# A cast of the second query tile on ScalarE, and new places for the work of a list scheduler, in a fused attention, feed-forward and expert kernel

## The chip, the cores and the metric

One core of a Trainium2 chip runs the whole program as one launch. A core has five engines that run side by side, each through its own instructions in the order in which the program gives them: TensorE (PE, matrix products; PEld are its weight loads), VectorE (DVE), ScalarE (ACT), GpSimd (POOL) and SyncE (SP, which here issues nearly all transfers). The DMA engines move the data. The metric is the device time of one execution in microseconds; the median of several runs is compared, lower is better.

## The reference

Three stages, each feeding the next:

```python
# 1. attention, batch 2, 8 heads, 576 tokens, head size 64, causal, with a bias from a running sum of s
cum = np.cumsum(np.maximum(s, 0.0), axis=-1)
bias = -(cum[:, :, :, None] - cum[:, :, None, :])
scores = np.where(causal, -1000000000.0, scale * np.matmul(q, k.transpose(0, 1, 3, 2)) + np.minimum(bias, 0.0))
attn = np.exp(scores - np.max(scores, axis=-1, keepdims=True))
x = np.matmul(attn / (np.sum(attn, axis=-1, keepdims=True) + 1e-09), v)      # 1152 tokens x 512
# 2. feed-forward, 512 -> 2048 -> 512
h = x @ w_in
x = (h * (1.0 / (1.0 + np.exp(-1.702 * h)))) @ w_out
# 3. eight experts: each token goes to the one with the largest logit, 512 -> 1024 -> 512 with relu
expert_idx = np.argmax(x @ w_gate, axis=1)
out[i] = gate_w[i] * (np.maximum(disp[e] @ w1[e], 0.0) @ w2[e])[pos[i]]
```

All inputs are float32. The kernel keeps most matrix products exact enough by splitting a number into a high and a low part and multiplying both.

## The kernel before, in words

Attention works on 8 head pairs x (2 batches of 4 pairs) and, in each pair, on 5 query tiles t: tile 0 has 64 rows, the others 128, and tile t sees 64 + 128 t keys. One `unit(x, t)` makes the scores of both heads of the pair on TensorE (`score_mm`, line 719, with the causal mask added at 720), their row maxima on VectorE, the exponentials `pexp` on ScalarE, and then splits `pexp` into two float16 parts in the tile `ph`: a cast gives the high part (`copy`, line 702 on ScalarE or 704 on VectorE, by the tuple PHA), and two subtractions on GpSimd (lines 764 and 769) give the low part. A DMA transpose on SyncE's queue (line 777) turns `ph` into `PT`; tiles 0 and 1 share the buffer `ph01` and one transpose. `av_unit` then multiplies PT with the split values V (line 797).

The operands of the scores lie in two buffers `QK[x % 2]`: rows 0 to 63 are the transposed k and q of the pair, made by `qk_T` from the loaded `kraw` and `qraw` (loaded by `qk_load`, line 667) with transposes on TensorE (688) and copies on ScalarE (694). Two further rows, 64 and 65, carry the running sums of s. For pair 0 they come straight from the prologue (`bias_rows`, line 535). The prologue also writes the sums of all pairs to `cum_d` in HBM (`bias_keep`, line 542), and for each later pair a small transfer in `qk_T` (line 677) reads them back into `QK`. `v_load` (594) loads v, `w_load` (358, 361) the weights of the dense stage, 512 KB at a time, three of them early.

The dense stage (`mm1`, `mm2`) begins inside attention and then fills TensorE alone; `w_conv` splits its weights. After it come routing (`logits`, `route`, `order`) and, for each expert, `w_unit` (weights), `xs_in`, `e_mm1`, `e_mm2` and `e_out`, which scatters the rows to the output.

The order of the work on every engine is made by the class `Plan`. Every step is given to `pl.op` with its engine, an estimate of its duration, what it reads and writes, and a rank. `Plan.run` plays the program with these estimates: on each engine, among the steps that are ready (or will be within 120 ns of the earliest), it takes the one with the lowest place, and this order is emitted. The place is the rank plus a number from the table `SHIFT`, which is looked up by a name made of the stage (a before rank 0, b0 to b4 for attention by rank modulo 5, b and c after it), the function, the engine and the buffer written. The rank in attention is 5 x + t. Transfers on SyncE and GpSimd are held back in this play while more than 3.18 us of earlier transfers are still to be done. The places change nothing in what is computed: dependencies hold under every order.

The ranks that the prediction speaks of: the v loads -20; `bias_keep` -9; `qk_load(1)` -10; `qk_load(2)` 2; the three early weight loads 1, 2 and 3; the bias rows of pair 1 and its transposes and copies 1; the transpose of tile t of pair x 5 x + t; the cast of tile 1 of pair x 5 x + 1.

Of the kernel before, what the change touches and what calls it, by code (L numbers as in the profile page):

```python
# [1610 lines left out]
```

## Time and profile before

| | us |
|---|---|
| median of 3 runs | 493.71 (492.6 to 497.37) |
| the profiled execution, its own time | 495.86 |
| its span, first to last instruction | 494.1 |
| TensorE busy in it | 465.5 |
| mean granted TensorE clock | 0.979 of 2.4 GHz |

The profile is of one execution; its times are microseconds from its first instruction. Matmuls overlap in the array, so that a busy TensorE is not one at its peak. The releaser of a wait is inferred, from the event that came last.

### The profile page before, as it was taken

How to read it: one execution, taken by the hardware profiler on the slowest of the kernel's cores; microseconds unless marked ns; L12 is line 12 of the kernel's file. 1: busy time of each engine (PE TensorE's matmuls, PEld its weight loads, DVE VectorE, ACT ScalarE, POOL GpSimd, SP SyncE). 2: the span in 40 equal slices, each digit the busy share in tenths (PEclk: the TensorE clock that was granted, in tenths of full speed). 3: DMA queues.
4: the chain of work that ended last, by engine and by line, in shares of the span. 5: the costliest groups of instructions: out<-in, count | busy, mean ns of one | idle time of the engine just before them, and what ended most of it. 6: DMA issues, size and time to landing. Idle time of an engine off the chain costs nothing.

```text
span 494.1 us, 9648 instructions
## 1 busy us (share of the span) xinstructions
PE 465.5 (94%) x3379; PEld 352.1 (71%) x3398; DVE 359.3 (73%) x817; ACT 328.6 (67%) x754; POOL 128.4 (26%) x136
## 2 busy tenths in 40 slices
PE   6599989999999999999999999999999999989993
PEld 5366666667677666766766966759688898878981
DVE  8867767888979988982324466846986879799980
ACT  3567878987557656673335346842886988899981
POOL 5616765867212222211000130002000110220250
PEclk9968989999999999999999999999999999999998
DMA  7997999978972554692000248821694687876820
GB/s 164 255 226 150 239 233 171 211 148 152 206 217 96 172 155 148 215 356 87 1 1 0 87 172 312 323 84 44 195 348 151 184 265 243 288 241 226 273 84 21
DMA packets 99047, 88.20 MB, mean 179 GB/s; under 512 B 66679, under 2 KB 77943, under 8 KB 98982
## 3 DMA queue, kind: packets, MB, share of 16 engines
q1 hardware_dynamic: 97108, 82.04, 61.3%
q0 software_dynamic: 1888, 5.52, 2.9%
q8 instruction: 27, 0.44, 0.4%
q14 instruction: 24, 0.20, 0.1%
HBM read 60.60 MB, written 14.19 MB: 151 GB/s over the span
## 4 chain that ended last, share of the span: by engine, by line
PE 49%; DMA 13%; DVE 12%; issue 10%; ACT 8%; POOL 5%; SPq 1%; POOLq 0%; DVEq 0%; ACTq 0%
PE SC L466 8%; PE SC L719 6%; PE MI L433 5%; DMA PT<-ph 5%; PE MX L433 4%; DMA out_dram<-x2R,small 4%; PE SC L467 3%; PE MI L437 2%; PE AV L1401 2%; PE AV L797 2%; PE MX L437 2%; DMA wraw<-in_moe_w_out_dram 2%; POOL ph L769 2%; PE MI L1372 2%; POOL ph L764 2%
## 5 line engine op out<-in xcount | busy, mean ns | idle before, releaser
L466 PE MATMUL SC<-woH,gtH 128*128 128x512 f32 x212 | 75.8, 481 | 0.0
L719 PE MATMUL SC<-QK 128*128 128x512 f32 (+4 forms) x192 | 65.1, 449 | 8.5 <-POOL ph L769 4.3
L447 DVE SCALAR_TENSOR_TENSOR gtH<-th,gtH 128x384 fp32r<-128x384 f32 x46 | 25.8, 561 | 40.0 <-ACT gtH L445 39.3
L764 POOL TENSOR_TENSOR ph<-pexp,ph 128x512 f16<-128x512 f32 (+4 forms) x32 | 44.7, 1398 | 31.8 <-DVE ph L704 26.3
L450 ACT ACTIVATE gtB<-th 128x384 bf16<-128x384 f32 x46 | 24.0, 521 | 37.1 <-PE SC L467 24.5
L433 PE MATMUL MI<-xT,wiH 128*128 128x384 f32 x216 | 47.0, 356 | 0.5 <-DVE th L443 0.4
L750 ACT ACTIVATE pexp<-SC,smA 128x192 f32<-128x192 f32 (+4 forms) x80 | 38.4, 520 | 12.7 <-DVE smA L741 9.2
L719 PEld LDWEIGHTS SC<-QK 128*128 128x128 f32 (+1 forms) x192 | 29.8, 197 | 23.1 <-issue 11.4
L466 PEld LDWEIGHTS SC<-woH,gtH 128*128 128x128 f32 x212 | 40.3, 194 | 3.2
L1295 DVE TENSOR_TENSOR wiL<-wraw,wiH 128x1024 bf16<-128x1024 f32 x32 | 38.9, 1221 | 3.7 <-ACT wiH L1294 3.5
L1295 DVE TENSOR_TENSOR woL<-wraw,woH 128x1024 bf16<-128x1024 f32 x32 | 38.9, 1218 | 3.1 <-ACT woH L1294 3.0
L1437 POOL DMA_INDIRECT out_dram<-x2R,small x8 | 9.9, 1240 | 119.1 <-ACT x2R L1464 82.5
L409 POOL TENSOR_TENSOR wiL<-wvi,wiH 128x512 bf16<-128x512 f32 x16 | 22.2, 1386 | 68.6 <-ACT wiH L405 64.2
L467 PEld LDWEIGHTS <-gtB 128*128 128x128 bf16 x138 | 13.2, 96 | 37.5 <-issue 37.2
L433 PEld LDWEIGHTS MI<-xT,wiH 128*128 128x128 f32 x216 | 37.8, 189 | 2.2 <-DVE th L443 0.9
L1118 POOL DMA_INDIRECT xs_d<-x2R,small x9 | 9.0, 996 | 112.9 <-DVE small L1058 57.3
L433 PE MATMUL MX<-xT,wiH 128*128 128x384 f32 x168 | 36.6, 358 | 0.1
L467 PE MATMUL SC<-woL,gtB 128*128 128x512 bf16 x94 | 36.7, 390 | 0.0
L1294 ACT ACTIVATE wiH<-wraw 128x1024 fp32r<-128x1024 f32 x32 | 33.6, 1055 | 1.9 <-DMA wraw<-in_moe_w_dram 1.4
L694 ACT ACTIVATE QK<-MI 64x288 f32<-64x288 f32 x57 | 24.1, 423 | 14.6 <-PE MI L688 9.0
L1294 ACT ACTIVATE woH<-wraw 128x1024 fp32r<-128x1024 f32 x32 | 33.5, 1055 | 0.4 <-DMA wraw<-in_moe_w_dram 0.4
L433 PEld LDWEIGHTS MX<-xT,wiH 128*128 128x128 f32 x168 | 29.6, 189 | 1.6 <-DVE th L443 0.8
(290 smaller groups left out, 1146.3 us busy)
## 6 DMA issues: line engine op xcount, KB each, us to landing
wraw<-in_moe_w_dram SPq DMA_DIRECT2D x64, 512.0 KB
wraw<-in_moe_w_in_dram SPq DMA_DIRECT2D x16, 512.0 KB
wraw<-in_moe_w_out_dram SPq DMA_DIRECT2D x16, 512.0 KB
xs_d<-x2R SPq DMA_DIRECT2D x16, 257.0 KB
kraw<-in_k_dram SPq DMA_DIRECT2D x8, 288.0 KB
qraw<-in_q_dram SPq DMA_DIRECT2D x8, 288.0 KB
out_dram<-x2R SPq DMA_DIRECT2D x9, 256.0 KB
x2R<-xs_d SPq DMA_DIRECT2D x8, 257.0 KB
```

The lines of the kernel that those rows point to most:

```text
L409: e_.tensor_tensor(out=dlo, in0=vi.bitcast(F32), in1=dhi.bitcast(F32), op=ALU.subtract)
L433: nc.tensor.matmul(ps, lhsT=whi[:, kc], rhs=xT[:, a, kc, cs], start=(kc == 0 and a == 0), stop=False)
L447: pl.op("dve", t_dve(CN), lambda: nc.vector.scalar_tensor_tensor(out=gh[:, 1], in0=th, scalar=0.5, in1=gh[:, 0].bitcast(F32), op0=ALU.mult ...
L450: pl.op("act", t_act(CN), lambda: nc.scalar.activation(out=gb, in_=th, func=AF.Copy, scale=0.5), r=[("th", n % 2)], w=[("gtb", gi)] + xw)
L466: nc.tensor.matmul(o, lhsT=gh[:, a, ts], rhs=whi, start=(fc == 0 and a == 0), stop=False)
L467: nc.tensor.matmul(o, lhsT=gb[:, ts], rhs=wlo, start=False, stop=(fc == NFC - 1))
L694: pl.op("act", t_act(3 * TQ, False) + 130, lambda o=o, in_=in_, sc=sc: nc.scalar.activation(out=o, in_=in_, func=AF.Copy, scale=sc), r=[bk ...
L719: nc.tensor.matmul(o[:rows, j0:j1], lhsT=t_[:, 2 * r, i0:i0 + rows], rhs=t_[:, 2 * r + 1, j0:j1], start=True, stop=False)
L750: pl.op("act", t_act(wdt, False, 1), lambda o=o, r=r, nm=nm: nc.scalar.activation(out=pe[:rows, r, :wdt], in_=o[:rows, :wdt], func=AF.Exp, ...
L764: pl.op(eng, (t_pool if eng == "pool" else t_dve)(n * T_), lambda rs_=rs_, e_=e_: e_.tensor_tensor(out=hl[:, rs_, 0:T_], in0=pe[:rows, rs_ ...
L1294: pl.op("act", t_act(1024), lambda: nc.scalar.activation(out=dhi, in_=raw, func=AF.Copy), r=[rk], w=kh, rank=rank, after=after)
L1295: pl.op("dve", t_dve(1024), lambda: nc.vector.tensor_tensor(out=dlo, in0=raw, in1=dhi.bitcast(F32), op=ALU.subtract), r=[rk, ks[0], ks[2]] ...
```

## The change

Two things change. PHA becomes (0, 1), so that the cast of tile 1 is done by ScalarE with `activation(Copy)` instead of VectorE with `tensor_copy`, once in each of the 8 pairs. And the table SHIFT is replaced: 255 entries become 377. Nearly every name has another number, and 122 entries have a suffix: a step's place is now its rank plus the entry of its name plus the entry of name and group, where the group of an attention step is its pair (`@0` to `@7`; `@x` for those with a rank of 40 or more) and that of a later step its rank divided by 12. Entries lie between -40 and 40 as before.

```diff
-    "a.bias_keep.sp.cumd": 3.9, "a.bias_rows.sp.QKb": -7.7, "a.consts.a.pool.identF": -19.5, "a.consts.b.pool.": 13.3,
...
-    "a.qk_T.act.QK": 9.4, "a.qk_T.dve.QK": -10.1, "a.qk_T.tr.pe.BK": 13.3, "a.qk_load.sp.raw": -15.6,
-    "a.v_load.sp.vraw": 14.3, "a.v_scale.dve.gtb": 34.4, "a.v_scale.dve.scl": 37.3, "a.v_scale.pe.BK": 16.3,
...
-    "b0.w_conv.top.act.wvi": -13.9, "b0.w_load.load.sp.wraw": 1.9, "b1.av_unit.pe.BK": 18.8, "b1.copy.dve.ph": 4.7,
-    "b1.qk_T.act.QK": -11.3, "b1.qk_T.sp.QKb": 24.3, "b1.qk_T.tr.pe.BK": -14.1, "b1.unit.act.pexp": -10.7,
...
-    "b1.unit.sp.PT": 2.2, "b1.v_load.sp.vraw": 6.1, "b1.w_conv.both.dve.wvi": -7.6, "b1.w_conv.low.dve.wraw": -12.9,
...
-    "b1.w_conv.top.act.wvi": -18.2, "b1.w_load.load.sp.wraw": 0.4, "b2.av_unit.act.xT": 8.7,
...
-    "b2.qk_load.sp.raw": -2.1, "b2.unit.act.pexp": -17.7, "b2.unit.dve.nm": -20.1, "b2.unit.pe.BK": 0.6,
-    "b2.unit.pool.phl": 14.7, "b2.unit.pool.phz": 32.1, "b2.unit.sp.PT": -19.6, "b2.v_load.sp.vraw": 2.3,
...
-    "b2.w_load.load.sp.wraw": 37.2, "b3.av_unit.pe.BK": 16.7, "b3.copy.dve.ph": -40, "b3.unit.act.pexp": -40,
...
-    "b3.unit.pool.phl": -19.8, "b3.unit.pool.phz": 18.2, "b3.unit.sp.PT": 35.9, "b3.v_load.sp.vraw": 19.8,
...
-    "b3.w_load.load.sp.wraw": 5.1, "b4.av_unit.act.xT": 12.4, "b4.av_unit.dve.ri": -3, "b4.av_unit.dve.xTl": 7.4,
...
-    "b4.unit.pe.BK": -0.8, "b4.unit.pool.phl": -30.2, "b4.unit.pool.phz": -22, "b4.unit.sp.PT": 39,
...
+    "a.bias_keep.sp.cumd": -10.7, "a.bias_rows.sp.QKb": -25, "a.consts.a.pool.identF": -16.4,
...
+    "a.qk_load.sp.raw": -13, "a.v_load.sp.vraw": 11.9, "a.v_scale.dve.gtb": -5.4, "a.v_scale.dve.scl": -24.6,
...
+    "b0.w_conv.top.act.wvi": 24.6, "b0.w_load.load.sp.wraw": -10.8, "b1.av_unit.pe.BK": -36.6, "b1.copy.act.ph": 39.5,
+    "b1.copy.act.ph@5": -8.7, "b1.qk_T.act.QK": -13.3, "b1.qk_T.act.QK@0": -13.3, "b1.qk_T.act.QK@2": 9.1,
...
+    "b1.qk_T.sp.QKb": -1.3, "b1.qk_T.tr.pe.BK": -31.4, "b1.qk_T.tr.pe.BK@1": 21.5, "b1.unit.act.pexp": -13.4,
...
+    "b1.unit.pool.phl@5": 17.6, "b1.unit.pool.phz": -11.2, "b1.unit.sp.PT": -17.2, "b1.v_load.sp.vraw": 10.5,
...
+    "b1.w_load.load.sp.wraw": -11.6, "b2.av_unit.act.xT": 22, "b2.av_unit.dve.ri": 3.9, "b2.av_unit.dve.ri@4": 2.9,
...
+    "b2.qk_load.sp.raw@3": 18.9, "b2.qk_load.sp.raw@4": 3.6, "b2.unit.act.pexp": -21, "b2.unit.dve.nm": 16.6,
...
+    "b2.unit.pool.phz@1": -22, "b2.unit.sp.PT": 19.9, "b2.v_load.sp.vraw": -9.4, "b2.w_conv.both.dve.wvi": -8.4,
...
+    "b2.w_conv.sign.dve.wvi": 0.7, "b2.w_conv.top.act.wvi": -28, "b2.w_load.load.sp.wraw": 21.5,
+    "b2.w_load.load.sp.wraw@0": 17.2, "b3.av_unit.pe.BK": 26.9, "b3.av_unit.pe.BK@3": 31.2,
...
+    "b3.unit.sp.PT": 1.2, "b3.unit.sp.PT@1": 1.2, "b3.v_load.sp.vraw": 10.3, "b3.v_load.sp.vraw@2": 15.7,
...
+    "b3.w_load.load.sp.wraw": 14.9, "b4.av_unit.act.xT": 24.2, "b4.av_unit.act.xT@2": 17.9, "b4.av_unit.dve.ri": -12,
...
+    "b4.unit.pool.phz@6": 8.2, "b4.unit.sp.PT": 17.1, "b4.v_load.sp.vraw": -8.4, "b4.w_conv.both.dve.wvi": -19.6,
...
         if rank is None:
             rank = self.rank
-        rank += SHIFT.get(self.name(eng, fn, w, rank), 0.0)
+        name = self.name(eng, fn, w, rank)
+        rank += SHIFT.get(name, 0.0) + SHIFT.get(name + self.group(name, rank), 0.0)
...
+    def group(self, name, rank):
+
+        return {"a": "@", "b": f"@{int(rank // 5)}" if rank < 40.0 else "@x", "c": f"@{int(rank // 12)}"}[name[0]]
...
     XTB = "act"
     AVG = (0, 3)
-    PHA = (0,)
+    PHA = (0, 1)
```

The entry of `b2.qk_load.sp.raw` in the new table is 15.3.

## Rows read from the trace of the kernel before

**Rows 1.** The page, part 1: busy time, share, instructions of each engine.
```profile
PE 465.5 (94%) x3379; PEld 352.1 (71%) x3398; DVE 359.3 (73%) x817; ACT 328.6 (67%) x754; POOL 128.4 (26%) x136
```

**Rows 2.** Busy time by stretch: stretch, length, engines (x instructions), granted clock, DMA, GB/s.
```profile
0.00:12.00 12.00, 7.93 (x68) 6.59 (x69) 9.87 (x22) 4.16 (x10) 6.73 (x25) 1.00 0.78 162
12.00:140.00 128.00, 115.69 (x1120) 80.50 (x1120) 101.49 (x217) 96.54 (x221) 74.25 (x71) 0.93 1.00 200
140.00:337.50 197.50, 196.93 (x1044) 139.49 (x1057) 125.29 (x267) 108.29 (x209) 23.99 (x21) 1.00 0.43 147
337.50:475.00 137.50, 134.28 (x1084) 117.83 (x1084) 116.24 (x295) 113.12 (x293) 20.58 (x16) 1.00 0.69 227
475.00:494.10 19.10, 10.63 (x77) 7.71 (x76) 6.40 (x18) 6.49 (x24) 2.89 (x3) 0.90 0.07 26
```

**Rows 3.** Waits of TensorE, 12 to 140 us: us in total, times, longest.
```profile
PE SC L719 <- POOL ph L769: 4.3, 1, 4.3
PE AV L797 <- DMA PT<-ph: 3.0, 4, 1.1
```

**Rows 4.** TensorE in order of time: start, us, what [idle before, releaser].
```profile
8.84 0.56 PE L719 MATMUL SC<-QK 128*128 128x192 f32 x2 [1.33 <-DMA QK<-QK]
...
19.89 0.47 PE L688 MATMUL MI<-identF,qraw 96*128 96x96 f32 x3 [0.64 <-ACT QK L694]
24.68 0.98 PE L719 MATMUL SC<-QK 128*128 128x192 f32 x2 [4.32 <-POOL ph L769]
```

**Rows 5.** ScalarE in order of time: the copies of q of the first head.
```profile
20.50 0.85 ACT L694 ACTIVATE QK<-MI 64x288 f32<-64x288 f32 x2
```

**Rows 6.** SyncE's queue in order of time.
```profile
13.46 0.44 SPq L358 DMA_DIRECT2D wraw<-in_moe_w_in_dram  x1
14.00 1.93 SPq L777 DMA_TRANSPOSE PT<-ph  x1
15.99 0.56 SPq L358 DMA_DIRECT2D wraw<-in_moe_w_in_dram  x1
16.66 1.68 SPq L677 DMA_DIRECT2D QK<-cum_d  x1
```

**Rows 7.** Instructions of line 677: duration in ns, least, median, most.
```profile
L677 SPq DMA_DIRECT2D QK<-cum_d x7: 261/298/1680, 16.7 to 95.9; - x7
```

**Rows 8.** Busy time by stretch, 4 us each, columns as in rows 2.
```profile
12.00:16.00 4.00, 4.00 (x18) 1.98 (x17) 3.60 (x9) 1.32 (x4) 1.62 (x2) 1.00 1.09 292
16.00:20.00 4.00, 2.85 (x18) 1.75 (x17) 3.44 (x10) 3.33 (x8) 3.54 (x4) 1.00 1.50 253
20.00:24.00 4.00, 0.36 (x3) 0.17 (x3) 3.47 (x6) 2.51 (x5) 2.89 (x3) 0.84 0.78 207
```

**Rows 9.** Busy time by stretch around the slow clock, columns as in rows 2.
```profile
23.00:24.00 1.00, 0.00 (x0) 0.00 (x0) 1.00 (x1) 0.00 (x0) 1.00 (x2) 0.50 1.09 286
31.00:32.00 1.00, 1.00 (x4) 0.55 (x2) 0.88 (x2) 0.96 (x4) 0.00 (x0) 0.50 1.14 185
33.00:34.00 1.00, 1.00 (x38) 1.00 (x35) 0.49 (x2) 0.00 (x0) 0.00 (x0) 1.00 1.32 241
43.00:47.00 4.00, 4.00 (x30) 3.31 (x30) 2.59 (x7) 2.15 (x7) 2.50 (x2) 0.57 0.87 203
70.00:74.00 4.00, 4.00 (x39) 3.39 (x39) 2.50 (x6) 1.48 (x5) 2.50 (x2) 0.57 1.27 265
```

**Rows 10.** Groups by line and shape, 0 to 145 us: busy us, mean ns, idle before.
```profile
L704 DVE CAST ph<-pexp 128x384 f16<-128x384 f32 x8 | 3.0, 377 | 0.4 <-ACT pexp L750 0.4
L702 ACT ACTIVATE xTb<-xT 128x320 bf16<-128x320 f32 x8 | 3.8, 470 | 0.3
L702 ACT ACTIVATE xTb<-xT 128x256 bf16<-128x256 f32 x8 | 3.3, 417 | 0.3
```

**Rows 11.** The page, part 4: shares of the chain that ended last.
```profile
PE 49%; DMA 13%; DVE 12%; issue 10%; ACT 8%; POOL 5%; SPq 1%; POOLq 0%; DVEq 0%; ACTq 0%
```

**Rows 12.** Busy time, 60 to 100 us, columns as in rows 2.
```profile
60.00:100.00 40.00, 35.70 (x382) 25.10 (x380) 31.15 (x75) 33.58 (x77) 27.78 (x25) 0.96 1.07 205
```

More of the change, by code (lines that the diff above doesn't have):

```diff
@@ L23 @@
 SHIFT = {
-    "a.bias_keep.sp.cumd": 3.9, "a.bias_rows.sp.QKb": -7.7, "a.consts.a.pool.identF": -19.5, "a.consts.b.pool.": 13.3,
-    "a.consts.dve.identB": -28.5, "a.consts.dve.ones1": 13.2, "a.consts.dve.ph": 22.6, "a.consts.dve.vss": 9.9,
-    "a.consts.pool.QKb": 1.4, "a.consts.pool.V2o": 22.6, "a.prologue.dve.cum": 6.7, "a.prologue.dve.neg": 5.3,
-    "a.prologue.dve.one": 16.1, "a.prologue.dve.one2": 25.2, "a.prologue.dve.s": 22, "a.prologue.sp.s": -32.6,
-    "a.qk_T.act.QK": 9.4, "a.qk_T.dve.QK": -10.1, "a.qk_T.tr.pe.BK": 13.3, "a.qk_load.sp.raw": -15.6,
@@ L29 @@
-    "a.v_load.sp.vraw": 14.3, "a.v_scale.dve.gtb": 34.4, "a.v_scale.dve.scl": 37.3, "a.v_scale.pe.BK": 16.3,
[3 rows of a table removed]
-    "b.w_conv.low.dve.wraw": -28.8, "b.w_conv.main.act.wo": -6.4, "b.w_conv.rest.dve.wo": -25.6,
-    "b.w_conv.rest.pool.wo": 9.4, "b.w_conv.sign.dve.wvi": -7.6, "b.w_conv.top.act.wvi": 21.5,
[38 rows of a table removed]
-    "c.evac.dve.x2r": -1.4, "c.expert.ld.sp.eid": -39.6, "c.first_early.dve.sel": 28.3, "c.first_early.mm.pe.BK": 3.6,
-    "c.first_load.load.sp.x2r": 2.4, "c.first_rows.dve.sel": 7.1, "c.first_rows.pe.BK": -23.5, "c.keep.pool.": 14.7,
@@ L75 @@
-    "c.keep.sp.": 12.5, "c.logits.act.x2T": 10.4, "c.logits.dve.ix": -4.3, "c.logits.dve.lg": 9.3,
-    "c.logits.dve.mx": 23.7, "c.logits.dve.x2T": -33.3, "c.logits.mm.pe.BK": -39.3, "c.logits.pe.BK": -21.9,
-    "c.mm1.act.gt": 9.5, "c.mm1.act.gtb": -5.4, "c.mm1.act.th": 25.2, "c.mm1.dve.gtl": -9.1, "c.mm1.dve.th": 6.7,
-    "c.mm1.pe.BK": -24.6, "c.mm2.mm.pe.BK": -17.6, "c.order.dve.base0": -4.2, "c.order.dve.ov": 13.3,
-    "c.order.dve.srt": 31.1, "c.pool.iotaW": 16.2, "c.route.act.w8": 9.2, "c.route.count.pe.BK": -31.8,
@@ L80 @@
-    "c.route.dve.cnt": 26.7, "c.route.dve.gate": -28.3, "c.route.dve.idx": -23.8, "c.route.dve.oc": -5.1,
-    "c.route.dve.oh": 11.4, "c.route.dve.pos": 17.9, "c.route.dve.rel": -28.6, "c.route.dve.sb": -20.2,
-    "c.route.dve.se": 0.4, "c.route.dve.slot": -28.1, "c.route.dve.t3": 35.2, "c.route.dve.tok": -21.3,
-    "c.route.dve.w8": -37.5, "c.route.scatter.pool.xs": -26.9, "c.send.scatter.pool.": -8.7,
-    "c.w_conv.both.dve.wvi": -25.3, "c.w_conv.low.dve.wraw": -5.6, "c.w_conv.main.act.wi": 18.5,
@@ L85 @@
-    "c.w_conv.main.act.wo": 10.2, "c.w_conv.rest.dve.wo": 14.8, "c.w_conv.rest.pool.wi": -11.5,
-    "c.w_conv.sign.dve.wvi": 20.1, "c.w_conv.top.act.wvi": 29.1, "c.w_load.load.sp.wraw": 22.9,
-    "c.w_unit.act.wi": 18.2, "c.w_unit.act.wo": 22.4, "c.w_unit.dve.wi": 7.8, "c.w_unit.dve.wo": 6.2,
-    "c.w_unit.load.sp.wraw": -0.7, "c.xs_first.act.xsT": -14.6, "c.xs_first.act.xsTb": -2.9,
-    "c.xs_first.dve.xsTb": 19.9, "c.xs_first.dve.xsTl": -0.3, "c.xs_first.load.sp.meta": -23.2,
-    "c.xs_in.act.xsT": -21.8, "c.xs_in.act.xsTb": 21.1, "c.xs_in.dve.meta": -18.5, "c.xs_in.dve.xsTl": 9.8,
@@ L91 @@
-    "c.xs_in.load.sp.x2r": -38.7, "c.xs_in.tr.pe.BK": -1.5, "c.zero.pool.zrow": -8.2, "c.zeros.sp.out0": -1.9,
-    "c.zeros.sp.xs0": 2.5,
+    "a.bias_keep.sp.cumd": -10.7, "a.bias_rows.sp.QKb": -25, "a.consts.a.pool.identF": -16.4,
+    "a.consts.b.pool.": -18.8, "a.consts.dve.identB": -8.4, "a.consts.dve.ones1": 3.2, "a.consts.dve.ph": 13.4,
+    "a.consts.dve.vss": 4, "a.consts.pool.QKb": -9.4, "a.consts.pool.V2o": -2.1, "a.prologue.dve.cum": 20.1,
+    "a.prologue.dve.neg": -8.5, "a.prologue.dve.one": -8.2, "a.prologue.dve.one2": 9.6, "a.prologue.dve.s": -19.4,
@@ new lines @@
+    "a.prologue.sp.s": -15, "a.qk_T.act.QK": 23.5, "a.qk_T.dve.QK": 8, "a.qk_T.tr.pe.BK": -17.9,
+    "a.qk_load.sp.raw": -13, "a.v_load.sp.vraw": 11.9, "a.v_scale.dve.gtb": -5.4, "a.v_scale.dve.scl": -24.6,
[3 rows of a table added]
+    "b.w_conv.both.dve.wvi": 19.4, "b.w_conv.low.dve.wraw": -8.3, "b.w_conv.low.dve.wraw@x": -22.1,
+    "b.w_conv.main.act.wo": -8.2, "b.w_conv.rest.dve.wo": -6.1, "b.w_conv.rest.pool.wo": 0.8,
+    "b.w_conv.sign.dve.wvi": 2.2, "b.w_conv.top.act.wvi": -5.9, "b.w_load.load.sp.wraw": 22.3, "b0.copy.act.ph": 30.1,
[59 rows of a table added]
@@ new lines @@
+    "c.first_early.mm.pe.BK": 39, "c.first_load.load.sp.x2r": 17.8, "c.first_rows.dve.sel": 12.7,
+    "c.first_rows.pe.BK": 8.9, "c.keep.pool.": 21, "c.keep.sp.": -10.7, "c.logits.act.x2T": 19.3,
[7 rows of a table added]
+    "c.route.count.pe.BK@2": 7.6, "c.route.dve.cnt": 3.7, "c.route.dve.gate": 3.1, "c.route.dve.idx": -17.9,
+    "c.route.dve.oc": -23, "c.route.dve.oh": -14.4, "c.route.dve.oh@3": 6.5, "c.route.dve.pos": -9.7,
+    "c.route.dve.rel": 22.2, "c.route.dve.sb": -30.2, "c.route.dve.se": -32.5, "c.route.dve.se@3": 21.8,
@@ new lines @@
+    "c.route.dve.slot": -12.2, "c.route.dve.t3": -0.3, "c.route.dve.tok": -31.5, "c.route.dve.w8": -9.2,
+    "c.route.scatter.pool.xs": -18, "c.send.scatter.pool.": 14.1, "c.w_conv.both.dve.wvi": -13.4,
+    "c.w_conv.low.dve.wraw": 19.2, "c.w_conv.main.act.wi": 19.5, "c.w_conv.main.act.wo": -15.1,
+    "c.w_conv.rest.dve.wo": 2.7, "c.w_conv.rest.dve.wo@0": 23, "c.w_conv.rest.pool.wi": 12.4,
+    "c.w_conv.sign.dve.wvi": 24.9, "c.w_conv.sign.dve.wvi@0": -10.8, "c.w_conv.sign.dve.wvi@2": -35.2,
@@ new lines @@
+    "c.w_conv.top.act.wvi": 18.6, "c.w_conv.top.act.wvi@1": -11.6, "c.w_load.load.sp.wraw": -4.2,
+    "c.w_load.load.sp.wraw@1": -6.6, "c.w_unit.act.wi": 27.5, "c.w_unit.act.wi@11": 4.7, "c.w_unit.act.wi@7": 0.9,
+    "c.w_unit.act.wi@8": -15.2, "c.w_unit.act.wo": 39.6, "c.w_unit.act.wo@10": 16.6, "c.w_unit.dve.wi": 8.7,
+    "c.w_unit.dve.wi@11": 11.2, "c.w_unit.dve.wo": 3.3, "c.w_unit.load.sp.wraw": 8.1,
+    "c.w_unit.load.sp.wraw@4": -23.2, "c.w_unit.load.sp.wraw@6": 6.3, "c.w_unit.load.sp.wraw@7": 22,
@@ L93 @@
+    "c.xs_first.act.xsT": -12.9, "c.xs_first.act.xsTb": 26.4, "c.xs_first.dve.xsTb": 5.6, "c.xs_first.dve.xsTl": -1.6,
[6 rows of a table added]
 }
```

94 rows, old and new, of the table SHIFT are left out of this document.

## The prediction

> **What bounds the kernel now.** I read the page's first part, then the busy time in five stretches, then TensorE's waits, and last the order of time around the longest of them. The reader is to see that TensorE is at work for 465.5 of 494.1 us [rows 1], so that nearly all that an order can give back lies in its 28.6 idle us and in its slow stretches. The five stretches [rows 2] say where these are: start-up 4.1 us idle (12.00 - 7.93), attention 12.3 us (128.00 - 115.69), the dense stage 0.6 us, routing and experts 3.2 us, the end 8.5 us. Attention is also the only long stretch in which the granted clock is below 1: 0.93. So attention is the stage to look at. The dense stage after it hardly waits at all; what attention saves should therefore reach the end of the kernel.
>
> Of the waits inside attention one is far longer than the others: a score matmul waits 4.3 us, once; four waits for a transposed tile make 3.0 us [rows 3]. In order of time it is the first score matmul of the second head pair (x = 1): TensorE ends its last transpose at 19.89 + 0.47 = 20.36 us and starts again at 24.68 [rows 4]. The row names POOL as the releaser, yet a score matmul reads nothing that POOL has just written. Its operands are QK, written by ScalarE, which had the first head's last part ready at 20.50 + 0.85 = 21.35 us [rows 5], and the two bias rows, which one small transfer (line 677) brings from cum_d. The SyncE queue issues that transfer at 16.66 us, behind two weight loads and the first transpose [rows 6], and the issue itself takes 1680 ns where the median of the seven is 298 [rows 7]. By elimination I take the bias transfer as what ended the wait, about 8 us after its issue: it stood behind a backlog.
>
> The bytes agree. By the shapes in the code, in KB, 36 (s), 576 (k and q of pair 0), 1152 (v), 18 and 144 (cum rows), 576 and 576 (k and q of pairs 1 and 2), 1024 (two weight loads) and 256 (the first transpose) go ahead of it: 4358 KB, 4.46 MB. The transfers moved 1.94 MB by 12 us (12 x 162 GB/s [rows 2]), then 1.17, 1.01 and 0.83 MB in 4 us each [rows 8]; 4.46 MB is reached at 21.6 us. The wait ended at 24.68, some 3 us later.
>
> The Trainium skill, "DMA: Bandwidth & Descriptors", section Queues, rings and completion order, says that on each DMA engine the descriptors of a queue are consumed in ring order, so that a small transfer does not pass what is ahead of it there; the 8 us here agree. [...]
>
> **The change, part by part.**
>
> *Places of the early transfers.* A place is rank plus shift, the lower going first among what is ready. For the bias rows of pair 1 it goes from 1 + 24.3 = 25.3 to 1 - 1.3 = -0.3. The first weight load goes from 1.4 to -10.6, the third from 8.1 to 17.9, the second from 39.2 to 40.7 (2 + 21.5 + 17.2); k and q of pair 2 from -0.1 to 17.3. The writing of cum_d goes from -5.1 to -19.7, past the v loads (-5.7 to -8.1). So cum_d is written earlier, and the bias rows then stand behind one weight load instead of two and ahead of k and q of pair 2: 4358 - 576 - 512 = 3270 KB, 3.35 MB, reached at 16.95 us, or 3.09 MB at 15.9 us if the first transpose comes later too. With the same 3 us behind it they land between 18.9 and 20.0 us. Late next is ScalarE's copy of q, done at 21.35. The signal from TensorE to this copy took 0.14 us (20.36 to 20.50); with as much on the way back TensorE starts at 21.5 instead of 24.68, 3.2 us earlier. If the copy also comes earlier (its place falls from -10.3 to -25.6, ahead of most exponentials) it is up to the whole 4.3 us; if the transfer was not the cause, 0. I take -3.2.
>
> *The slow stretch behind the wait.* At the end of the idle time the granted clock is 0.50 (1.2 GHz), still so at 31 us, and 1.00 again at 33 [rows 9]; two score matmuls of 192 columns take 0.98 us there against 0.56 at full clock [rows 4]. TensorE works at most 7.8 us in it (24.68 to 32.5), which at 0.56/0.98 would be 4.5 us: 3.3 us to gain at most, nothing at least. The shorter gap that is left may still cost some clock, since behind waits of at most 1.1 us [rows 3] the clock fell too, to a mean of 0.57 over the 4 us from 43 and from 70 us [rows 9]. I take half: -1.6.
>
> *The cast of the second query tile.* Eight casts of 128x384 leave VectorE, 377 ns each, 3.0 us [rows 10]. On ScalarE no row has this size; copies of 320 and 256 elements take 470 and 417 ns, 0.83 ns an element, so 384 take about 523 ns, 8 x 0.523 = 4.2 us (estimate). All of it on the path would be +4.2, all of VectorE's on it -3.0. Weighted by the share of the chain that each engine has, 8% and 12% [rows 11], it is +0.34 - 0.36: 0. What hides it is that TensorE sets the pace; without that cover it costs up to 4.2 us.
>
> *Transposes and all other places in attention.* The transposes of t = 1, 3 and 4 move forward by 19.4, 34.7 and 21.9, that of t = 2 back by 39.5, k and q back by at least 17.4. The four waits for transposes are worth 3.0 us, and the slow stretches at 43 and 70 us another 2 x 4 x (1 - 0.57) = 3.4 [rows 9]: 6.4 us, to be gained or doubled. Forward and back nearly balance; I take -0.4.
>
> *Places in the dense and expert stages.* Nearly every name moves. There are 0.6 and 3.2 us to gain [rows 2], and an order that fits worse could lose as much again. I take -0.3.
>
> Sum: -3.2 - 1.6 + 0 - 0.4 - 0.3 = -5.5 us. The profiled execution took 495.86 us (its span of 494.1 and 1.8 around it), which gives 490.4; it lay 2.15 us above the median of 493.71, so against that median 488.2 us.
>
> **Rivals.**
>
> *The lead is eaten.* The DMA engines' share over attention is 1.00 [rows 2]. If transfers set the pace over the whole stage, an early start of pair 1 only waits longer later, at the transposes. For it: the share, 1.07 between 60 and 100 us [rows 12]. Against it: only 3.0 us of waits name a transfer. Then the time is 493. The Trainium skill ("Trainium Kernel Development and Optimization", section Key Constraints) states that all queues run on the same 16 DMA engines and interleave, so an order adds no bandwidth; by that rule this rival would hold wherever the engines are full.
>
> *The wait stays.* If POOL, as the row says, or something else ended it, the order on SyncE's queue changes nothing: 493.7.
>
> *The cast comes late (slower).* Its place on ScalarE is 1 + 39.5, behind nearly all that ScalarE has ready, and ScalarE is busy 33.58 of 40 us between 60 and 100 [rows 12]. Behind the cast wait POOL's subtractions of this tile, the transpose that serves t = 0 and 1, whatever SyncE has queued behind that, and TensorE's first attention-value matmuls. A cast of 0.52 us behind one piece of 0.9 us would be 1.4 us late in each of eight pairs: 11.4 us, less the 5.5 of the sum: 499.6. It decides from 5.5/8 = 0.7 us a pair on. Against it: a pair takes 16 us (128 us of attention over eight), and only a lateness that outlasts the work between the two pairs reaches TensorE.
>
> *More gaps close.* Half of attention's other 8 us of idle time and half of the experts' 3.2: 488.2 - 5.6 = 482.6.
>
> **How the numbers follow.** Forecast 0.42 (its own range 485.5 to 490.5), lead eaten 0.20, wait stays 0.07, cast late 0.16, more gaps close 0.15. About 1% is what a measurement of this kernel can tell from no change: 488.8 and 498.6. Of the forecast's 0.42 two thirds lie below 488.8, which with 0.15 makes 0.43 faster; of the late cast 0.15 lies above 498.6; the rest, 0.42, is within 1%. The range 481 to 496 leaves out the late cast and little below.
>
> **What would show it.** Right: in the new profile the bias rows' transfer is issued before 15 us and pair 1's first score matmul starts near 21.5, with an idle time before it of 1 to 1.5 us; the clock between 24 and 32 us is mostly 1; VectorE's eight 128x384 casts are gone and ScalarE has eight near 523 ns; attention's idle time is some 8 us. Wrong: a wait of 3 us or more remains there, waits for transposed tiles grow beyond 3.0 us in all, or TensorE's idle time between 140 and 475 us grows beyond 3.8 us.

## The result

The changed kernel took **488.88 us** (median of 13 runs, 487.55 to 494.02) where the kernel before, run beside it, took 494.06 us (median of 13, 491.76 to 500.02): ratio **0.9909, 95% interval 0.9885 to 0.9932**. In a second series it was 490.74 us against 494.08, ratio 0.9926 (0.9892 to 0.9959). So the gain is 3.7 to 4.5 us: clear of no change, just under 1%, and smaller than the 5.5 us of the sum. Some executions fell into a slower state, over 1.5% above the fastest of their kernel; ratios and intervals leave them out and medians do not, so that a ratio need not be the quotient of the two medians beside it. The profiled execution took 490.40 us, 488.7 of them its span.

**The profile after.** First the page's part 1 (busy time, share, instructions), then the five stretches, with the columns of rows 2. Lines of the kernel lie 36 further on: the scores are now L755, the bias transfer L713, the attention-value matmuls L833.

```profile
PE 460.2 (94%) x3379; PEld 349.9 (72%) x3398; DVE 358.2 (73%) x809; ACT 330.9 (68%) x762; POOL 128.2 (26%) x136
```

```profile
0.00:12.00 12.00, 8.39 (x72) 6.69 (x72) 8.69 (x21) 4.41 (x10) 6.87 (x25) 1.00 0.81 162
12.00:140.00 128.00, 114.67 (x1131) 79.84 (x1131) 107.32 (x217) 99.62 (x230) 71.46 (x71) 0.96 0.97 206
140.00:337.50 197.50, 196.26 (x1051) 140.32 (x1065) 121.37 (x275) 108.02 (x210) 24.26 (x21) 1.00 0.42 143
337.50:475.00 137.50, 134.93 (x1100) 119.25 (x1100) 118.85 (x293) 115.95 (x304) 23.76 (x18) 1.00 0.69 226
475.00:488.70 13.70, 5.94 (x38) 3.78 (x34) 1.94 (x7) 2.88 (x11) 1.85 (x2) 0.90 0.10 37
```

The reader is to see what did not change. TensorE's idle time is 488.7 - 460.2 = 28.5 us, against 28.6 before [rows 1]. Attention's is 13.3 us, against 12.3 [rows 2]. Nearly the whole difference between these two executions is in busy time: 5.3 us less, of which the granted clock accounts for at most (1 - 0.979) x 494.1 - (1 - 0.987) x 488.7 = 4.0; at most, because a slow clock costs nothing while TensorE waits.

Next, the place to which the prediction pointed. SyncE's queue, then TensorE, each in order of time:

```profile
11.46 0.45 SPq L394 DMA_DIRECT2D wraw<-in_moe_w_in_dram  x1
12.03 0.29 SPq L713 DMA_DIRECT2D QK<-cum_d  x1
```

```profile
20.70 0.47 PE L724 MATMUL MI<-identF,qraw 96*128 96x96 f32 x3 [1.04 <-ACT QK L730]
21.00 0.52 PE L755 MATMUL SC<-QK 128*128 128x192 f32 x2
...
23.99 0.32 PE L833 MATMUL AV<-V,PT 128*128 128x64 f16 x3 [1.80 <-DVE V L693]
```

The transfer is issued at 12.03 instead of 16.66 us [rows 6], pair 1's first score matmul starts at 21.00 instead of 24.68 [rows 4], without a wait. But 1.2 us later TensorE stands again, for 1.80 us, this time for V's split on VectorE. The waits between 12 and 140 us (us in total, times, longest) confirm it:

```profile
PE AV L833 <- DVE V L693: 3.7, 3, 1.8
PE AV L833 <- DMA PT<-ph: 2.8, 3, 1.4
```

In place of the 4.3 us of rows 3 there are now 3.7 us for V; the waits for transposed tiles are as before. The slow clock behind the wait got shorter, but did not go away (columns of rows 2; compare rows 9):

```profile
22.00:23.00 1.00, 0.19 (x2) 0.08 (x2) 1.00 (x1) 1.00 (x3) 1.00 (x1) 0.50 2.10 204
27.00:28.00 1.00, 1.00 (x19) 1.00 (x17) 1.00 (x3) 0.95 (x2) 0.00 (x0) 0.50 1.24 235
...
29.00:30.00 1.00, 1.00 (x28) 1.00 (x26) 1.00 (x2) 0.81 (x4) 0.00 (x0) 1.00 0.69 143
```

The casts are where they were expected, at 508 ns each (estimate 523), with no idle time of ScalarE before them:

```profile
L738 ACT ACTIVATE ph<-pexp 128x384 f16<-128x384 f32 x8 | 4.1, 508 | 0.0
```

From this profile alone one would say: forecast met, by the early transfer, but for attention's idle time, forecast at some 8 us. The experiments say otherwise.

### The profile page after: what moved, and what is told of

Same layout as the page of the kernel before. It is cut to its first block, busy times and chain, and to the rows that moved or that the text cites. A ratio compares the mean times of both kernels' runs of the same rounds, so it can differ in the third digit from the quotient of the medians.

```text
span 488.7 us, 9679 instructions
## 1 busy us (share of the span) xinstructions
PE 460.2 (94%) x3379; PEld 349.9 (72%) x3398; DVE 358.2 (73%) x809; ACT 330.9 (68%) x762; POOL 128.2 (26%) x136
## 4 chain that ended last, share of the span: by engine, by line
PE 65%; DVE 9%; DMA 8%; issue 6%; ACT 6%; POOL 3%; SPq 2%; POOLq 0%; DVEq 0%; ACTq 0%
PE SC L502 9%; PE AV L1437 7%; PE MI L469 5%; PE MX L469 5%; PE SC L503 4%; PE MI L1408 4%; PE MX L1408 4%; PE AV L1439 3%; DMA wraw<-in_moe_w_dram 3%; PE SC L755 3%; DMA PT<-ph 3%; PE AV L502 3%; PE MI L473 2%; PE MX L473 2%; POOL ph L800 2%
## 5 line engine op out<-in xcount | busy, mean ns | idle before, releaser
L755 PE MATMUL SC<-QK 128*128 128x512 f32 (+4 forms) x192 | 62.9, 432 | 4.0 <-ACT pexp L786 2.8
L786 ACT ACTIVATE pexp<-SC,smA 64x64 f32<-64x64 f32 (+4 forms) x80 | 37.9, 520 | 17.3 <-DVE smA L777 15.0
L502 PEld LDWEIGHTS SC<-woH,gtH 128*128 128x128 f32 x212 | 39.9, 194 | 3.0
L755 PEld LDWEIGHTS SC<-QK 128*128 128x128 f32 (+1 forms) x192 | 28.0, 186 | 16.3 <-issue 7.7
L833 PE MATMUL AV<-V,PT 128*128 128x65 f16 (+1 forms) x640 | 25.7, 197 | 6.5 <-DVE V L693 3.7
```

The source lines that it names most:

```text
L502: nc.tensor.matmul(o, lhsT=gh[:, a, ts], rhs=whi, start=(fc == 0 and a == 0), stop=False)
L755: nc.tensor.matmul(o[:rows, j0:j1], lhsT=t_[:, 2 * r, i0:i0 + rows], rhs=t_[:, 2 * r + 1, j0:j1], start=True, stop=False)
L786: pl.op("act", t_act(wdt, False, 1), lambda o=o, r=r, nm=nm: nc.scalar.activation(out=pe[:rows, r, :wdt], in_=o[:rows, :wdt], func=AF.Exp, ...
L833: nc.tensor.matmul(av[:, slot, r, 0:D + 1 - h_], lhsT=PT[t][:, r * (1 + 2 * t) + pb, :], rhs=rhs, start=(i == 0), stop=(i == len(m) - 1))
```

## The experiments

Twelve kernels in four series, each run 6 to 12 times beside the kernel before, whose median was 493.5 to 494.9 us.

| kernel | us | ratio to before (95%) |
|---|---|---|
| early_transfer: before + early transfer | 497.79 | 1.0035 (0.9999 to 1.0072) |
| cast_alone: before + cast on ScalarE | 495.65 | 1.0007 (0.998 to 1.0034) |
| attention_part: new places up to the end of attention | 492.48 | 0.9959 (0.9937 to 0.9981) |
| later_part: new places behind attention | 494.51 | 0.9997 (0.997 to 1.0024) |
| undo_early: changed, transfer late again | 489.55 | 0.9911 (0.9875 to 0.9946) |
| undo_cast: changed, cast on VectorE | 491.17 | 0.9939 (0.9905 to 0.9973) |
| undo_both: changed, both undone | 491.46 | 0.9950 (0.9922 to 0.9979) |
| unlock: changed, V split off POOL's subtraction | 491.02 | 0.9942 (0.9915 to 0.9968) |
| changed_again | 490.74 | 0.9926 (0.9892 to 0.9959) |
| first_pairs: new places up to pair 1 only | 499.44 | 1.0096 (1.0063 to 1.0128) |
| later_pairs: new places of pairs 2 to 7 only | 507.02 | 1.0224 (1.0177 to 1.0271) |
| routing_experts: new places of routing, experts only | 533.31 | 1.0747 (1.0708 to 1.0787) |

**One part alone, in the old order.** Two kernels keep every other instruction where the kernel before had it. In the first, a hook takes instructions out of the finished order; `put(n, m)` sets n right behind m:

```diff
+        put(at("sp", ("cumd", 0)), rows[1])
+        put(at("sp", ("cumd", 1)), at("sp", ("cumd", 0)))
...
+        put(loads[0], q1[3])
+        put(at("sp", ("QKb", 1, 0)), loads[0])
```

> The kernel before with every instruction in its old place but four steps of SyncE's queue: cum_d is written ahead of three v loads, and the first weight load and then the bias rows of pair 1 are issued ahead of k and q of pair 2 (the queue's order in the changed kernel, up to the first transpose). Theory 1 (this transfer carries attention's gain): pair 1's first score matmul starts near 21.5 us instead of 24.68 and the kernel is 2.5 to 4.8 us shorter, ratio 0.990 to 0.995. Theory 2 (the lead is used up by the second pair, as in the changed kernel, where it fell from 4.7 us at pair 1 to 1.2 us at pair 2, and attention's gain comes from other places): the first score matmul is early all the same, but the kernel is 0 to 1.2 us shorter, ratio 0.9975 to 1.000. If the wait stays near 24.7 us, the transfer was not its cause.

```diff
-            pl.op("dve", t_dve(n, True), lambda: nc.vector.tensor_copy(out=o, in_=i), r=r, w=w)
+            pl.op("dve", t_dve(n, True), lambda: nc.scalar.activation(out=o, in_=i, func=AF.Copy) if w[0] == ("ph", 1)
+                  else nc.vector.tensor_copy(out=o, in_=i), r=r, w=w)
```

> The kernel before with every instruction in its old order; only the eight 128x384 casts are issued on ScalarE, at the place in the whole order at which VectorE had them. My theory (what one engine gains the other loses, and TensorE sets the pace): within 1 us of before, ratio 0.998 to 1.002. Rival (VectorE is on the path behind the scores): up to 3.0 us shorter, ratio 0.994. Rival (the casts delay the exponentials behind them on ScalarE): 8 times 0.51 us = 4.1 us longer, ratio 1.008.

The cast moves nothing (+0.3 us, -1.0 to +1.7). The early transfer alone moves nothing or costs a little (+1.7 us, 0 to +3.6). Why it brings nothing is seen in the two traces side by side: TensorE in cast_alone, whose SyncE queue is the old one, then in early_transfer.

```profile
20.63 0.47 PE L688 MATMUL MI<-identF,qraw 96*128 96x96 f32 x3 [0.63 <-ACT QK L694]
23.23 0.56 PE L720 MATMUL SC<-QK 128*128 128x192 f32 x2 [2.14 <-DMA QK<-cum_d]
```

```profile
21.07 0.47 PE L710 MATMUL MI<-identF,qraw 96*128 96x96 f32 x3 [0.64 <-ACT QK L716]
22.63 0.56 PE L741 MATMUL SC<-QK 128*128 128x192 f32 x2 [1.09 <-issue]
```

The first row pair names the transfer as what ends the wait; that part of the reasoning holds. But the wait is 2.1 us here, 1.8 in later_part and 3.0 in later_pairs (below), whose queue up to this transfer is the same, not 4.3: the profile of before had caught a long one. With the transfer early, 1.09 us remain, ScalarE's copy of q (21.68 + 0.85 = 22.53 us) being what comes late next, as the prediction had it. The start moves by 0.4 to 0.6 us.

**One half of the places, by stage.** The cast and the table's entries for start-up and attention with the old entries behind them, and the converse:

```diff
+SHIFT = {k: v for k, v in CHANGED.items() if k[0] in "ab"}
+SHIFT.update({k: v for k, v in BEFORE.items() if k[0] == "c"})
```

CHANGED and BEFORE stand for the two tables, and in the kernel the result is written out; in the converse they change places, and the cast stays on VectorE.

> The changed kernel's cast and its places of start-up and attention, with the old places for the dense, routing and expert stages. In the changed kernel attention's end lies 3.1 us ahead of before, and the stages behind it give 2.3 us more. Theory A (the stages add up, since the dense stage hardly waits): 3.1 us shorter than before, ratio 0.9937, and no more. Theory B (an earlier and differently loaded end of attention is what the later stages gained from): the whole 5.4 us, ratio 0.989. Theory C (the later stages lose what attention gains without their own new places): ratio 0.998 or more.

> The other half: the old places of start-up and attention and the old cast, with the changed kernel's places for the dense, routing and expert stages. Theory A (the stages add up): 2.3 us shorter than before (dense -0.6, routing +1.0, experts +1.3, end +0.6), ratio 0.9953. Theory B (the later gain comes from attention's end): within 0.5 us of before, ratio 0.999 to 1.001. As predicted before the change ran it would be 0.3 us shorter.

Attention's places bring 2.0 us (0.9 to 3.1), a ratio between Theory A's and Theory C's that settles neither. Alone, the later ones bring nothing (Theory A's 0.9953 lies outside the interval), though routing and experts in that profile were as short as in the changed kernel: its dense stage was longer, and in the 4 us from 284 on its clock fell, which the changed kernel's did not (later_part, then the changed kernel; columns of rows 2).

```profile
284.00:288.00 4.00, 3.75 (x15) 2.44 (x15) 1.21 (x10) 0.60 (x1) 1.94 (x2) 0.63 0.53 199
```

```profile
284.00:288.00 4.00, 4.00 (x22) 2.56 (x21) 1.69 (x14) 0.82 (x2) 1.83 (x2) 1.00 0.53 198
```

**One part undone, in the new order.** The changed kernel's order with the bias rows late again; with the casts on VectorE; and with SyncE's whole start as in the kernel before and the casts on VectorE.

```diff
+        put(at("sp", ("QKb", 1, 0)), loads[1])
```

> The changed kernel with its order kept, except that the bias rows of pair 1 are issued behind the second weight load, as in the kernel before; their writing to cum_d stays early. Theory 1 (pair 1's early bias rows carry attention's gain): pair 1's first score matmul starts 1.5 to 3 us later than 21.5 us and the kernel is 2 to 3.3 us longer than the changed one, ratio to before 0.995 to 0.998. Theory 2 (what the early start gains is used up by pair 2; the earlier runs speak for it: the transfer alone gave 1.0035): the first score matmul is late all the same, but the kernel stays within 1 us of the changed one, ratio 0.989 to 0.993.

```diff
-            pl.op("act", t_act(n), lambda: nc.scalar.activation(out=o, in_=i, func=AF.Copy), r=r, w=w)
+            pl.op("act", t_act(n), lambda: nc.vector.tensor_copy(out=o, in_=i) if w[0] == ("ph", 1)
+                  else nc.scalar.activation(out=o, in_=i, func=AF.Copy), r=r, w=w)
```

> The changed kernel with its order kept, except that the eight 128x384 casts are issued on VectorE at the same place in the whole order. Theory (the engine of the cast doesn't matter while TensorE sets the pace; the cast alone gave 1.0007): within 1 us of the changed kernel, ratio 0.989 to 0.993. Rival (the casts on ScalarE carry the gain, because VectorE delays POOL's subtractions and the V split): 2 us longer or more, ratio 0.995 or more.

> The changed kernel itself, for the same chip and session as the runs beside it: 0.9885 to 0.9932 as in its first measurement. Were it near 0.996, the changed places behind attention would be worth nothing here either (attention's part alone gave 0.9959, the later part alone 0.9997); near 0.991, they are worth about 0.5% behind the new attention and nothing behind the old one.

Its 0.9926 lies between the two values that this expectation sets against each other, so it does not decide what the places behind attention are worth.

undo_both is undo_cast's edit and these:

```diff
+        put(at("sp", ("cumd", 0)), raws[3])
...
+        put(raws[5], raws[4])
+        put(loads[0], raws[5])
+        put(at("sp", ("QKb", 1, 0)), loads[1])
```

> The changed kernel with its order kept, except that SyncE's queue has the order of the kernel before from its start to the bias rows of pair 1 (cum_d behind all v loads, k and q of pair 2 and two weight loads ahead of the bias rows) and that the eight 128x384 casts are issued on VectorE. What is left of the change are the places of all other instructions. Theory (the early transfer and the cast carry nothing; the places of the other instructions, which only work together, carry the whole gain): within 1.5 us of the changed kernel, ratio to before 0.989 to 0.996, and pair 1's first score matmul late (23.5 us or more) with the lead gone by pair 2. Rival (transfer and cast matter together, each covering for the other): 0.997 or more.

undo_early is the clearest, since its profile starts like that of the changed kernel (see the last section). Pair 1's first score matmul is late by 2.6 us again, and by pair 2 it is all one. VectorE's split of V, then TensorE, in undo_early (at 23.64 pair 1's first score matmul, at 39.75 the first 64-row one of pair 2):

```profile
21.50 2.66 DVE L709 SCALAR_TENSOR_TENSOR V<-vraw,misc,V 128x512 f16<-128x512 f32 x1 [0.25 <-ACT V L707]
```

```profile
23.64 0.98 PE L771 MATMUL SC<-QK 128*128 128x192 f32 x2 [2.26 <-POOL ph L816]
...
25.25 0.40 PE L849 MATMUL AV<-V,PT 128*128 128x65 f16 x4
...
38.94 0.59 PE L849 MATMUL AV<-V,PT 128*128 128x65 f16 x14
...
39.75 0.33 PE L771 MATMUL SC<-QK 128*64 128x64 f32 x2
```

The same in the changed kernel (its start stands in the section on the result):

```profile
21.27 2.67 DVE L693 SCALAR_TENSOR_TENSOR V<-vraw,misc,V 128x512 f16<-128x512 f32 x1 [0.25 <-ACT V L691]
```

```profile
38.66 0.59 PE L833 MATMUL AV<-V,PT 128*128 128x65 f16 x14 [0.79 <-DMA PT<-ph]
...
39.46 0.33 PE L755 MATMUL SC<-QK 128*64 128x64 f32 x2
```

The lead is used up at two places. V's split ends at 24.16 us in undo_early and at 23.94 in the changed kernel: in undo_early TensorE comes to the matmuls that need it at 25.3 us and does not wait, in the changed kernel it waits 1.80 us until 23.99, and 1.3 us of the lead are left. At 38.66 the changed kernel waits 0.79 us for a transposed tile and undo_early does not, and 0.3 us are left. The kernel as a whole loses nothing (0.9911; against the changed kernel beside it -1.2 us, -2.6 to +0.2, an estimate from the executions of both).

In undo_both one sign of the expectation failed: pair 1's first score matmul was to start at 23.5 us or later.

```profile
22.21 0.56 PE L778 MATMUL SC<-QK 128*128 128x192 f32 x2 [0.52 <-DMA QK<-cum_d]
```

In the profiled execution the old order of the queue, with the transfers issued from 16.74 us on, cost a wait of 0.52 us, so this kernel takes away the early issue, but little of the early start. With the transfer and the cast both undone, 0.9950 is left: the places of the other instructions alone give 2.5 us (1.0 to 3.9). Whether the rest, 1 to 2 us, belongs to transfer and cast together, the intervals do not say, since 0.9950 (0.9922 to 0.9979) and 0.9926 (0.9892 to 0.9959) overlap.

**The new wait taken away.** Pair 0's last cast, and what depends on it, behind the first V split:

```diff
+        last = at("dve", ("V2", 0, 0))
+        moved = [at("dve", ("ph", 4))]
...
+        for n in moved:
+            put(n, last)
+            last = n
```

> The changed kernel with one place more moved: the first V split of 128x512 on VectorE stands ahead of the cast of pair 0's last query tile, so that POOL's subtraction of this tile (2.1 us) no longer runs at the same time. In the changed kernel this split took 2.67 us where later ones take 0.74, and TensorE waited 1.8 us for it. Theory (the split was long because POOL worked beside it): the split takes 0.7 to 1.0 us, the wait at 22 us falls below 0.5 us. If the time saved there reaches the end, 1.3 to 3 us less than the changed kernel, ratio 0.985 to 0.988; if a lead of this stage is used up by pair 2 as the early transfer's was, the same as the changed kernel, 0.990 to 0.992. Rival (the split is long for another reason): it stays above 2 us.

VectorE, POOL and TensorE in this kernel:

```profile
21.78 0.75 DVE L715 SCALAR_TENSOR_TENSOR V<-vraw,misc,V 128x512 f16<-128x512 f32 x1 [1.41 <-ACT V L713]
...
23.91 2.54 DVE L715 SCALAR_TENSOR_TENSOR V<-vraw,misc,V 128x512 f16<-128x512 f32 x1
```

```profile
23.78 2.12 POOL L822 TENSOR_TENSOR ph<-pexp,ph 128x1024 f16<-128x1024 f32 x1
```

```profile
26.50 1.42 PE L855 MATMUL AV<-V,PT 128*128 128x64 f16 x23 [1.76 <-DVE V L715]
```

The first split takes 0.75 us as the theory said. The second now runs beside POOL's subtraction, takes 2.54, and TensorE waits 1.76 us at 24.7 instead of 1.80 at 22.2. The wait was moved, not removed, and the time stayed (0.9942 against 0.9926 beside it).

**Where in attention.** The new table for start-up and pairs 0 and 1 with the old one for all the rest, and for pairs 2 to 7 only:

```diff
-        rank += SHIFT.get(name, 0.0) + SHIFT.get(name + self.group(name, rank), 0.0)
+        table = FIRST if name[0] == "a" or name[0] == "b" and rank < 10.0 else SHIFT
+        rank += table.get(name, 0.0) + table.get(name + self.group(name, rank), 0.0)
```

> The changed kernel's places for start-up and the first two head pairs alone (and its cast), the old places for pairs 2 to 7 and all behind. In the profiles so far the slow stretch of TensorE's clock around 22 to 34 us cost 3.4 us (time times one minus the granted clock) in all six kernels with the new attention order, and 5.2 us in three of the four with the old one. Theory X (attention's gain is this shorter slow stretch): here too 3.4 us, and the whole of attention's gain, 1.8 to 2.0 us, ratio to before 0.9955 to 0.997. Theory Y (the gain lies in pairs 3 to 6, where the new order needs 37 to 39 us from the first score of pair 3 to that of pair 6 and the old one 46 to 50): the same as before, ratio 0.998 to 1.002.

> The converse: the old places for start-up and the first two head pairs, the changed kernel's places for pairs 2 to 7, the old ones behind attention (with the new cast). Theory X (the shorter slow stretch at 22 to 34 us is attention's gain): the slow stretch costs 5.2 us here and the kernel is the same as before, ratio 0.998 to 1.002. Theory Y (the gain lies in pairs 3 to 6): 37 to 39 us from pair 3's first score to pair 6's, and 1.8 to 2.0 us shorter than before, ratio 0.9955 to 0.997.

Both kernels are slower than before, by 4.7 and 11 us. That speaks against Theory X; Theory Y was not put to the test, since in later_pairs pair 3's first 64-row score to pair 6's takes 46.5 us (54.51 to 101.00), as in the old order. Theory X's sign is there in first_pairs: over the 20 us from 20 on the granted clock is 0.83, as in the changed kernel, and 0.74 in later_pairs, as in the kernel before (first_pairs, then later_pairs; columns of rows 2).

```profile
20.00:40.00 20.00, 16.09 (x145) 11.13 (x144) 16.60 (x34) 16.74 (x38) 8.61 (x10) 0.83 1.06 206
```

```profile
20.00:40.00 20.00, 16.43 (x139) 11.40 (x139) 15.37 (x29) 14.48 (x32) 8.84 (x9) 0.74 0.99 203
```

It did not help: the shorter slow stretch is (0.83 - 0.74) x 20 = 1.8 us of clock, and first_pairs gives that back, and more, to waits: TensorE is idle for 16.1 us between 12 and 140 us, against 12.3 before. Here are TensorE's of first_pairs between 12 and 140 us, then two of later_pairs in the whole span:

```profile
PE AV L866 <- DMA PT<-ph: 5.2, 6, 1.5
PE SC L788 <- ACT pexp L819: 3.3, 9, 0.9
...
PE AV L866 <- DVE V L726: 1.9, 1, 1.9
```

```profile
PE AV L866 <- DMA PT<-ph: 6.3, 5, 2.4
...
PE SC L788 <- DMA QK<-cum_d: 3.0, 1, 3.0
```

**Routing and experts alone.** The kernel before with only these entries new:

```diff
+DENSE = ("c.mm1", "c.mm2", "c.w_conv", "c.w_load")
+SHIFT = {k: v for k, v in BEFORE.items() if k[0] in "ab" or k.startswith(DENSE)}
+SHIFT.update({k: v for k, v in CHANGED.items() if k[0] == "c" and not k.startswith(DENSE)})
```

> The kernel before with the changed places of routing and experts alone; the second batch's dense matmuls, weight loads and conversions keep the old ones. In every profile with the new places behind attention the stretch from the last dense matmul to the first expert matmul took 10.4 to 10.5 us (old 11.4 to 11.7), and from there to the last expert matmul 124.3 to 126.2 us (old 126.9 to 127.9), 3.2 us in all by the means; yet the later part alone gave 0.9997. Theory (in that kernel the dense stage lost what routing and experts gained: its clock fell to 0.63 at 284 to 288 us, which the old and the changed kernel don't show): here the dense stage keeps its time and the kernel is 2 to 3.2 us shorter, ratio 0.9935 to 0.996. Rival (these landmarks are the scatter of single executions): ratio 0.998 to 1.002.

It missed by 40 us. Routing's last counts come only at 346 us, behind the last dense matmul, and then everything waits for the tokens to be gathered (TensorE, whole span):

```profile
PE MI L1019 <- DMA x2R<-xs_d: 12.8, 2, 9.0
```

The expectation treated the places of a stage as if each had a worth of its own. The three kernels with tables mixed inside a stage show that they have not: a place says only who goes first among what is ready, and with other neighbours the same place gives another order.

## Why the prediction came out right, and where its reasons did not

The time and the sign were right (488.2 forecast, 488.88 measured), the size nearly (5.5 us against 3.7 to 4.5). The reasons were right as to the mechanism at 20 us and wrong as to what it is worth: the largest term, -3.2, is 0 as far as the runs can tell, and the two smallest, -0.7 together, carry most of the gain. That the sum came out is luck.

*The early transfer (-3.2).* This step failed as a price. What it says of the trace came true: issue before 15 us (12.03), first score near 21.5 (21.00), an idle time of 1 to 1.5 us (1.04, though before the last transposes of q and not before the score). But the gain of a start was carried to the end of the kernel unchanged. Alone it gave 0 to +3.6 us; undone in the changed kernel it cost nothing. Two errors: the 4.3 us came from one execution, where kernels with the same queue show 3.0, 2.1 and 1.8 and undo_both 0.5; and of what is late next only ScalarE's copy was looked up. Behind it stood V's split, which TensorE's first attention-value matmuls need: with the scores at 21.00 TensorE waits 1.80 us for it, with the scores at 23.64 not at all, and a transposed tile at 38.66 us took most of the rest.

*The slow stretch (-1.6).* The size of the stretch is near (in both profiles' clock between 20 and 40 us, 0.74 against 0.83: 1.8 us), its worth is not shown, and "the clock between 24 and 32 us is mostly 1" was wrong: it was 0.50 until 28. And the cause was another: the stretch is as short in undo_early and undo_both, whose transfer is late. What the kernels with the new attention order share is that TensorE's first attention-value matmuls come between 21.95 and 25.25 us, in the old order between 26.80 and 29.36. That this shortened the stretch is only argued, for cast_alone, in the old order, has the short one too (columns of rows 2):

```profile
20.00:40.00 20.00, 16.26 (x142) 10.87 (x142) 17.20 (x35) 16.47 (x37) 10.47 (x11) 0.83 0.96 212
```

cast_alone took as long as before (1.0007) and first_pairs longer, so the shorter stretch alone is not the gain.

*The cast (0).* Right: 508 ns each, nothing alone (1.0007), and undone 0.4 us more than the changed kernel beside it (491.17 against 490.74), where the executions of the two allow -1.3 to +2.0 (estimate). The slower rival, a late cast, did not come.

*Places in attention (-0.4) and behind (-0.3).* These terms were too small: between them the places carried 2.5 us (1.0 to 3.9) without transfer and cast; attention's part with both gave 2.0 (0.9 to 3.1). The forecast balanced names moved forward against names moved back, which says nothing about an order. Where it shows: from pair 3's first 64-row score to pair 6's the new attention order takes 37 to 39 us in seven profiles, the old one 46 to 50 in five; 6 us of that are given back before attention ends, 2.3 us earlier by the means (138.3 against 140.6, routing_experts left out), some of it by the mix of the two kinds of start told of below. Nor is the shorter stretch the gain by itself: first_pairs has 39.9 us there and is slower than before.

The stages behind differ as clearly. From the end of the last dense matmul to the end of the program the seven profiles with the changed table there take 153.5 to 155.4 us, the six with the old one 157.0 to 158.3, among them attention_part (routing_experts left out). That later_part's 0.9997 shows nothing of it goes with its dense stage, 198.5 us from attention's end to the last dense matmul's in its profile against 195.9 before, and with the clock: its executions have a mean granted clock of 0.9782, those of the kernel before in that series 0.9811, those of attention_part 0.9845. As time times one minus the clock, the most that a slow clock can cost, that is 1.5 us more for later_part and 1.7 less for attention_part, which could be nearly all that this half gained. So the two halves do not tell which of the two terms was the larger error.

*The rivals.* "The lead is eaten" described the early lead better than the forecast did, but only in the smaller part by its mechanism: a transposed tile took 0.79 us of it, V's split more; in all, the waits for transposed tiles did not grow (2.8 against 3.0 us), and the DMA engines' share fell to 0.97. "The wait stays" is refuted: the rows name the transfer. "TensorE idle between 140 and 475 us" stayed at 3.8 us, as before. "More gaps close" did not come: attention's idle time grew by 1.0 us.

**What stays open:** which places make the gain, within attention or behind it, how much of it is the granted clock, and whether transfer and cast together add the last 1 to 2 us. Orders that differ in one named part and agree in all else would be needed; mixed tables do not make them.

## What to carry to other kernels

A wait at the start of a long pipelined stage is worth what is left of it at the stage's end: follow a lead over the next two waits, on every engine, before adding it to a sum. To price one move in a scheduled kernel, hold the emitted order and move that instruction alone, in both directions; changing one entry of a table of places changes the whole order, and a part of a fitted table can cost more than the whole brings (here up to 37 us). And before a forecast rests on one wait, ask whether another execution of the same code shows the same wait: here 4.3, 3.0, 2.1 and 1.8 us.

## What was not expected of the hardware

**The same kernel starts in two ways.** TensorE at the start of the changed kernel, first in the profile above, then in a second one of the same kernel:

```profile
6.43 1.17 PE L586 MATMUL SC<-onesB 128*128 128x128 bf16 x18
...
10.04 0.54 PE L755 MATMUL SC<-QK 128*128 128x192 f32 x2
```

```profile
6.80 2.13 PE L586 MATMUL SC<-onesB 128*128 128x128 bf16 x18
...
10.04 1.01 PE L755 MATMUL SC<-QK 128*128 128x192 f32 x2
```

In the second the matmuls take nearly twice as long until about 14 us, as long as behind the wait at 24 us where the granted clock is 0.50 (0.99 us for the same pair), though the row of 8 to 12 us gives it as 1.00:

```profile
8.00:12.00 4.00, 4.00 (x22) 3.10 (x21) 1.15 (x5) 0.82 (x3) 0.00 (x0) 1.00 0.90 185
```

That column says nothing here: the trace of this execution lists granted clocks only from 14.45 us on, that of the first from 4.69, and the view takes the time ahead of the list as 1.00. The durations decide, and they turn fast where the list begins. All fourteen profiles of this study start slow (the first 24 matmuls take 2.74 us in each); seven are fast by 6 us (two of them, undo_cast and routing_experts, slow again for some us from 11 us on), five by 10.6, and two, this one and first_pairs, by 14.5. Both kinds occur in either order of attention.

In this second profile pair 1's first score starts at 23.31 instead of 21.00 us, pair 2's first 64-row score at 43.16 instead of 39.46, and the span is 491.1 instead of 488.7 us. That the 2.4 us at the end are those of the start is not shown, since slow stretches came at other places in between. But a landmark of one profile, set against one of another, can be off by half of the whole gain. It is also part of why the wait of rows 4 was long: before's profile is fast early, and TensorE was ready at 20.36 us, in cast_alone at 21.10; the rest is that the wait for the transfer ended 1.5 us later (24.68 against 23.23).

**A VectorE instruction more than three times as long beside POOL.** V's split of 128x512 takes 0.74 to 0.75 us, and 2.67 (2.54 in unlock) when POOL's subtraction of 2.12 us starts with it; moving it away from POOL moved the long duration to the split that came next to POOL instead. The Trainium skill, "SBUF — State Buffer", section Who interferes with whom, says that a VectorE instruction with two SBUF inputs contends with a GpSimd instruction that reads SBUF, for a port pair that one of them holds to its end. These rows agree: the split beside POOL ends at 26.45 us, 0.55 us after the subtraction (25.90), as if it had mostly waited for it, and the same 0.55 lies between their ends in the changed kernel (23.94 and 23.39).
